# First blocks of a sliding-window attention and MLP kernel: q and k loaded and turned by batch, g applied at the copy of xT, w1 loaded ahead of two v blocks

## The chip, the cores and the metric

The kernel runs on one core of a Trainium2 chip. The metric is the device time of one execution in microseconds; the time of a kernel is the median of several runs. All times in the text are microseconds unless marked otherwise, and times of events are counted from the start of the profiled span.

## The reference

Inputs are q, k and v of shape (8, 8, 576, 64) (batch, heads, positions, head size), a gain g of 512 numbers, and two weights, w1 (512 x 2048) and w2 (2048 x 512), all f32.

```python
scores = scale * np.matmul(q, k.transpose(0, 1, 3, 2))
rel = pos[:, None] - pos[None, :]
slopes = 2.0 ** (-8.0 * (np.arange(H) + 1) / H)
bias = slopes[:, None, None] * (-np.abs(rel))[None]
mask = (rel >= 0) & (rel < 128)
scores = np.where(mask, scores + bias[None], -1e9)
attn = softmax(scores)                      # over the keys
x = (attn @ v).transpose(0, 2, 1, 3).reshape(B, S, 512)
mu, var = mean(x), variance(x)              # over the 512 columns
xn = (x - mu) / np.sqrt(var + 1e-6) * g_ln
out = x + np.maximum(xn @ w_ch1, 0.0) @ w_ch2
```

## The kernel before

The batches are taken in four pairs. A pair has nine blocks of 128 rows: blocks 0 to 7 alternate between the two batches of the pair (block 2i + b holds positions 128i to 128i + 127 of batch b), and block 8 holds the last 64 positions of both. The 36 blocks form twelve groups for the MLP, six of two blocks and six of four (`GROUPS`). A block passes through these stages:

- *Load.* `load_qk` and `load_v` issue DMAs from GpSimd's queue that also convert f32 to f16. For the first pair the q and k of blocks 2i and 2i + 1 come as one tile `raw`, batch 0 in the lower 64 partitions and batch 1 in the upper 64, by one DMA each of 128 KB. The list `loads` fixes their order; `load_until` issues them as far as a step asks for. w1 comes in eight chunks of 256 columns (`load_w1`), w2 in four.
- *Turn.* q and k are transposed on TensorE in 64x64 pieces (`transposed`, line L297), and copied from PSUM to the tiles `q` and `k`. Later pairs are turned by DMA instead.
- *Scores.* `attend` (L425) multiplies q by the keys of the own and the preceding block of the same batch into one of two score banks (`ps_sc`); ScalarE takes the exponential (L434), VectorE multiplies by a mask with the decay (L445).
- *Values.* `values` (L479) multiplies by v with a column of ones, in two halves of four heads; VectorE takes the reciprocal of the sums and scales (L487, L488), which gives x, and the sum of each row.
- *Centre and turn x.* `centre` subtracts the mean. For blocks 0 to 3 it also multiplies by g, with g spread over all partitions in `g_row` (L554); for later blocks it only subtracts (L563). `turn_x` transposes the result on TensorE (L575) and copies it into the group's `xT` (L576), by ScalarE or VectorE as the step says.
- *MLP.* `mlp1` runs 16 units, each four matmuls with a 128-column slice of w1 (L737) and an eviction with relu by ScalarE (L753) or, for the units listed, by VectorE (L745). Unit u of the first groups takes columns 128u to 128u + 127, so chunk c of w1 serves units 2c and 2c + 1. Groups 0 and 1 (blocks 0 to 3) use plain `w1`, since g is already in x; later groups use `w1g`, made by VectorE from w1 and g (`gain_w1`, L163). `mlp2` multiplies by w2 (L770), and `finish` scales by the inverse standard deviation and adds x.

`g_row` comes from `turn_first`: g is loaded as one line of 512, spread over 128 partitions by a matmul of a line of ones (`spread_g`, L284, tile `ps_g`), and copied out of PSUM by VectorE (L364).

The order is written out by hand: the engines run in the program's order. `steps` is a list of small steps; the steps before `first` run ahead of the MLP, and `weave_at` puts later ones between the units of `mlp1` and `mlp2`: a place u means that one step is taken after unit u. `warm(n)` puts n matmuls of ones (L279) into TensorE's queue; their result is not used.

```python
steps = warm_step(11) + [[(turn_first,)]] + warm_step(3)
steps += [scores_step(0), scores_step(1) + masks_of(0) + masks_of(1)] + warm_step(6)
...
weave_at(mlp1(0, (0, 1)), 0, 1, 2, 3, 6, 7, 8, 12)
weave_at(mlp1(1), 2, 8, 12)
weave_at(mlp2(0, ((0, 8), (8, 12), (12, NFB))), 0, 1, 3, 4, 4, 5)
```

During `mlp1(1)` the steps are the statistics of blocks 0 to 3 (`variance_of`, with `inv_std` at the end) and 13 of the 16 instructions of `gain_w1`; the first step in `mlp2(0)` is the turn of blocks 4 and 5 ("turn(4)"), whose two copies on VectorE stand behind them.

Of the kernel before, what the change touches and what calls it, by code (L numbers as in the profile page):

```python
# [10 lines left out]
FP16 = mybir.dt.float16  # L11
# [6 lines left out]
P = 128  # L18
# [41 lines left out]
def kernel(  # L60
# [154 lines left out]
    def load_qk(src, tag, p, i):  # L215

        n = min(P, S - i * P)
        t = raw_pool.tile([P, H, 2, D], FP16, tag=tag, name=tag)
        raw[tag, p, i] = t
# [28 lines left out]
    weights = {3: w1s + w2s[:2], 5: w2s[2:] + [(load_distances,)]}  # L248
    loads, place = [], []
    for n, (p, blk) in enumerate(order):  # L250
        for src, tag in ((q, "q"), (k, "k")):
            sooner = tag == "q" and 0 < blk < T and by_dma(p, blk // 2)
            if blk % 2 == 0 and not sooner:
# [27 lines left out]
    def spread_g():  # L281

        ps = ps_mm.tile([P, DM], FP32, tag="mm", name="ps_g")
        nc.tensor.matmul(ps, one_line, g_line, start=True, stop=True)  # L284
        return ps

    def transposed(tag, p, i, ps):


        st = raw.pop((tag, p, i))  # L290
        for hp in range(HP):
            for r in range(2):
                for b, dst in enumerate(ps):
# [9 lines left out]
    def turn(p, i, in_sc=False, copies=(nc.vector.tensor_copy, nc.scalar.copy)):  # L303
# [16 lines left out]
        if i < 4:  # L320
            transposed("q", p, i, [t[:, 0] for t in ps])
            if p == 0 and i == 1:
                warm(3)
# [216 lines left out]
    def centre(p, blk):  # L540
# [28 lines left out]
    def turn_x(g, at, p, blk, copy):  # L569
# [6 lines left out]
        copy(out=xT[:, :, at * P : (at + 1) * P], in_=ps)  # L576
# [371 lines left out]
    nc.vector.memset(one_line, 1.0)  # L948
# [59 lines left out]
```

## Time and profile before

| | us |
|---|---|
| median of three runs | 307.76 (307.71 to 307.97) |
| the profiled execution | 306.61 |
| its span | 304.8 |
| TensorE busy | 296.6 |
| VectorE busy | 218.7 |
| ScalarE busy | 171.8 |
| GpSimd busy | 145.7 |
| first matmul of `mlp1(0)` | 17.84 |

PE is TensorE's matmuls and PEld its loads of weights, DVE is VectorE, ACT ScalarE, POOL GpSimd and SP the queue of the sync engine. In the timeline a row gives the start, the time taken, the engine, the line, the operation, output and inputs by their names, shapes, and the number of instructions merged; in brackets stands the idle time before it and what ended it. In the chain in order of time a row is a piece of the one chain of work that ended last. A row of the DMA view gives what is loaded, the queue, the number, the size and the time from issue to landing. GpSimd's DMA rows show the writing of descriptors, not the transfer.

### The profile page before, as it was taken

To read this page: it belongs to the slowest core of one execution; us is meant where nothing else is said; L and a number is where in the kernel's file an instruction comes from. 1 tells how busy PE (TensorE), PEld (TensorE's weight loads), DVE (VectorE), ACT (ScalarE), POOL (GpSimd) and SP (SyncE) were. 2 spreads that over 40 slices of the span, in tenths; PEclk is the share of its full clock that TensorE was granted. 3 is DMA by queue.
4 is the path that set the end of the run, shared out by engine and by line. 5 is a ranking of instruction groups with operands and counts; after the bars stand their busy time and mean duration, and the time that the engine had idled before them with its cause. 6 is when DMAs were issued, how large, how long until landed. Compare 5 with 4: busy or idle time off the path is not lost.

```text
span 304.8 us, 8795 instructions
## 1 busy us (share of the span) xinstructions
PE 296.6 (97%) x3625; PEld 199.2 (65%) x3625; DVE 218.7 (72%) x529; ACT 171.8 (56%) x302; POOL 145.7 (48%) x195
## 2 busy tenths in 40 slices
PE   8999999999999999999999999999999999999994
PEld 2468755856758576546865686568657864784583
DVE  2689778867688778757994899489858985760463
ACT  5598776768758476387248624762586257305600
POOL 8964658936399757535875357508210321000001
PEclk9999999999999999999999999999999999999998
DMA  9999999999999999999999999998752050021004
GB/s 96 163 196 202 189 184 158 192 129 139 177 162 134 152 147 139 154 183 146 119 162 215 134 118 152 141 178 68 148 109 54 19 156 19 18 88 69 2 0 138
DMA packets 160186, 39.25 MB, mean 129 GB/s; under 512 B 149073, under 2 KB 155729, under 8 KB 160146
## 3 DMA queue, kind: packets, MB, share of 16 engines
q0 software_dynamic: 109744, 18.65, 86.8%
q1 hardware_dynamic: 50178, 19.71, 41.4%
q8 instruction: 28, 0.46, 0.7%
q10 hardware_dynamic: 224, 0.33, 0.3%
q14 instruction: 12, 0.10, 0.2%
HBM read 36.97 MB, written 9.44 MB: 152 GB/s over the span
## 4 chain that ended last, share of the span: by engine, by line
PE 86%; DVE 5%; DMA 5%; ACT 1%; issue 1%; POOL 1%; DVEq 0%; POOLq 0%
PE ps_r L737 28%; PE ps_r L836 24%; PE ps_m L737 10%; PE ps_m L770 10%; PE ps_sc L425 5%; DMA xT<-xc 3%; PE ps_r L479 3%; PE ps_warm L279 2%; DMA out_dram<-o 2%; PE ps_pv L479 2%; PE ps_sc L297 1%; DVE x L488 1%; PE ps_tx L575 1%; DVE o L854 1%; POOL rstd L538 0%
## 5 line engine op out<-in xcount | busy, mean ns | idle before, releaser
L737 PEld LDWEIGHTS <-w1g 128*128 128x128 f16 x640 | 61.0, 98 | 48.5 <-issue 0.9
L737 PE MATMUL ps_r<-xT,w1g 128*128 128x512 f16 x384 | 84.8, 379 | 0.0
L434 ACT ACTIVATE probs<-ps_sc 128x1024 f16<-128x1024 f32 x56 | 54.3, 1023 | 51.0 <-PE ps_sc L425 51.0
L753 ACT ACTIVATE ht<-ps_r 128x512 f16<-128x512 f32 x96 | 56.1, 600 | 32.0 <-PE ps_r L737 31.8
L535 POOL TENSOR_TENSOR rstd<-moments,powers 128x1 f32<-128x1 f32 x28 | 13.8, 492 | 84.3 <-DVE moments L581 84.2
L770 PE MATMUL ps_m<-w,ht 128*128 128x512 f16 x192 | 45.3, 380 | 0.0
L836 PE MATMUL ps_r<-w,ht 128*128 128x256 f16 x384 | 43.9, 273 | 0.0
L836 PEld LDWEIGHTS <-ht 128*128 128x128 f16 x384 | 37.2, 98 | 4.7
L240 POOL DMA_DIRECT2D vx<-in_v_dram x40 | 34.9, 883 | 10.3 <-DMA k<-in_k_dram 3.5
L753 ACT ACTIVATE ht<-ps_m 128x256 f16<-128x256 f32 x91 | 33.1, 389 | 7.8 <-PE ps_m L737 4.9
L737 PE MATMUL ps_m<-xT,w1g 128*128 128x256 f16 x256 | 30.4, 273 | 0.8 <-ACT ht L753 0.6
L227 POOL DMA_DIRECT2D q<-in_q_dram x30 | 25.6, 859 | 9.5 <-DMA vx<-in_v_dram 5.8
L770 PEld LDWEIGHTS <-ht 128*128 128x128 f16 x192 | 17.3, 98 | 18.2
L227 POOL DMA_DIRECT2D k<-in_k_dram x30 | 25.8, 870 | 5.8 <-DMA q<-in_q_dram 3.9
L445 DVE TENSOR_TENSOR probs<-probs,m 128x1024 f16<-128x1024 f16 x44 | 27.8, 672 | 0.0
L580 DVE BATCH_NORM_STATS2 st<-x 128x6 f32<-128x512 f16 x36 | 24.8, 689 | 0.7
L538 POOL TENSOR_TENSOR rstd<-rstd,powers 128x1 f32<-128x1 f32 x28 | 22.7, 811 | 2.2
L487 DVE RECIPROCAL rec<-ps_r 128x4 f32<-128x4 f32 x36 | 6.3, 176 | 22.4 <-PE ps_r L479 22.3
L836 PE MATMUL ps_r<-w,hs 128*128 128x256 f16 x192 | 21.9, 273 | 0.0
L479 PEld LDWEIGHTS <-probs 128*128 128x128 f16 x448 | 18.7, 97 | 4.8 <-DVE probs L445 0.5
L854 DVE TENSOR_TENSOR o<-ps_r,o 128x512 f32<-128x512 f32 (+1 forms) x25 | 16.6, 666 | 5.5 <-PE ps_r L836 5.1
L836 PEld LDWEIGHTS <-hs 128*128 128x128 f16 x192 | 18.8, 98 | 2.2
(86 smaller groups left out, 361.9 us busy)
## 6 DMA issues: line engine op xcount, KB each, us to landing
out_dram<-o SPq DMA_DIRECT2D x22, 256.0 KB, 5.0
q<-in_q_dram POOLq DMA_DIRECT2D x32, 128.0 KB, 9.5
k<-in_k_dram POOLq DMA_DIRECT2D x32, 128.0 KB, 9.5
vx<-in_v_dram POOLq DMA_DIRECT2D x32, 128.0 KB, 9.3
out_dram<-o SPq DMA_DIRECT2D x24, 128.0 KB, 4.7
w<-in_moe_w_ch_dram POOLq DMA_DIRECT2D x8, 256.0 KB, 8.4
w<-in_moe_w_ch_dram POOLq DMA_DIRECT2D x4, 512.0 KB, 10.7
q<-in_q_dram POOLq DMA_DIRECT2D x8, 64.0 KB, 5.9
```

The lines of the kernel that those rows point to most:

```text
L227: nc.gpsimd.dma_start(out=dst, in_=rows.rearrange("h p d -> p h d"))
L240: nc.gpsimd.dma_start(out=vx[p0 : p0 + n, :, 0:D], in_=v[b, :, t0 : t0 + n, :].rearrange("h p d -> p h d"),)
L434: nc.scalar.activation(out=dst.rearrange("p (n j) q -> p j n q", j=2), in_=ps.rearrange("p j n t q -> p j n (t q)"), func=AF.Exp, scale=in ...
L445: nc.vector.tensor_tensor(out=dst, in0=dst, in1=mask, op=ALU.mult)
L479: nc.tensor.matmul(ps[:, i, :], pr[:, h, t, :], vext[(p * NSLOT + o) % NV][:, h, :], start=(n == 0), stop=(n == len(terms) - 1),)
L538: nc.gpsimd.tensor_tensor(out=here, in0=here, in1=powers[:, 1:2], op=ALU.pow)
L580: nc.vector.bn_stats(out=st, in_=xs[order[n]])
L737: nc.tensor.matmul(ps[:, 0:cols], w[:, kb, fb * P : (fb + 1) * P], xT[:, kb, 0:cols], start=(kb == 0), stop=(kb == NKB - 1),)
L753: nc.scalar.activation(out=ht[:, fb, 0:cols], in_=ps[:, 0:cols], func=AF.Relu)
L770: nc.tensor.matmul(sums[at], ht[:, fb, at * P : (at + 1) * P], w2[:, fb, :], start=(fb == 0), stop=(fb == NFB - 1),)
L836: nc.tensor.matmul(banks[name][pair][:, pair, :], lhs[:, fb, pair * P : (pair + 1) * P], rhs[:, fb, :], start=(first and fb == 0 and (pair ...
L854: nc.vector.tensor_tensor(out=o[:, at, cols], in0=banks[name][at.start][:, at, :], in1=(x if to_x else o)[:, at, cols], op=ALU.add,)
```

## The change

Four things change, all in the work on blocks 0 to 3.

1. `load_qk` can load one batch of a tile. The q and k of blocks 0 and 1 are loaded in the order q of batch 0, k of batch 0, q of batch 1, k of batch 1, and turned in that order by `turn_part` and `copy_part`, each batch in its own score bank. Blocks 2 and 3 are turned in two parts, q and then k. The steps of the head are written anew, with 29 warm-ups in place of 35.
2. `spread_g`, the line of ones and the load of g as a line are gone. `centre` only subtracts the mean; `turn_x` multiplies by g while it copies: on VectorE with one `tensor_tensor`, on ScalarE with four activations with a scale by partition. Block 0 is copied by ScalarE, blocks 1, 2 and 3 by VectorE (before: block 1 by VectorE, the others by ScalarE).
3. The first three chunks of w1 are loaded ahead of v of block 2, the fourth ahead of v of block 3, the other four behind it as before.
4. `mlp1(0)` has units 0 to 3 evicted by VectorE (before: 0 and 1), and nine steps woven in at other units (one half of the scores of block 2 moves behind `first`).

```diff
-    spread = hsum[1].rearrange("p f d -> p (f d)").bitcast(FP32)
-    g_line, g_row = spread[:, 0:DM], spread[:, DM : 2 * DM]
-    g_line = g_line[0:1]
-    nc.sync.dma_start(out=g_line, in_=moe_g_ln.rearrange("(o d) -> o d", o=1))
-    one_line = consts.tile([1, P], FP32)
...
-    def load_qk(src, tag, p, i):
+    def load_qk(src, tag, p, i, bs=range(2)):
...
-        for b in range(2):
+        for b in bs:
             nc.gpsimd.dma_start(
                 out=t[b * n // 2 : (b + 1) * n // 2],
...
-    weights = {3: w1s + w2s[:2], 5: w2s[2:] + [(load_distances,)]}
-    loads, place = [], []
+    weights = {3: w1s[4:] + w2s[:2], 5: w2s[2:] + [(load_distances,)]}
+    loads, place = [(load_qk, src, tag, 0, 0, (b,)) for b in range(2) for src, tag in ((q, "q"), (k, "k"))], []
...
+        loads += {2: w1s[:3], 3: w1s[3:4]}.get(n, [])
         loads.append((load_v, p, blk))
...
-    def turn_first():
-
-        q, k = queries(0, 0), keys_tile("k", 0, 0)
-        ps = [bank(b)[:, 0] for b in range(2)]
-        transposed("q", 0, 0, ps)
-        for b in range(2):
-            nc.vector.tensor_copy(out=q[:, b], in_=ps[b])
-        ps_row = spread_g()
-        warm(2)
-        ps = [bank(b)[:, 0] for b in (0, None)]
-        transposed("k", 0, 0, ps)
-        for b, copy in enumerate((nc.scalar.copy, nc.vector.tensor_copy)):
-            copy(out=k[:, b].rearrange("p h (c r) -> p r h c", r=2), in_=ps[b])
-        nc.vector.tensor_copy(out=g_row, in_=ps_row)
+    def in_score_bank(tag, b):
+
+        junk[b] = True
+        return ps_sc[b][:, "qk".index(tag)].bitcast(FP16).rearrange(
+            "p (t r h c) -> p t r h c", t=2, r=2, h=HP
+        )[:, 0]
+
+    def turn_part(tag, i, bs):
+
+        if (tag, 0, i) not in turned:
+            queries(0, i) if tag == "q" else keys_tile(tag, 0, i)
+        transposed(tag, 0, i, [in_score_bank(tag, b) for b in bs], bs[0])
+
+    def copy_part(tag, i, b, copy):
+        t, ps = turned[tag, 0, i][:, b], in_score_bank(tag, b)
...
+        copy(out=t, in_=ps)
...
-        if p == 0 and blk < FIRST:
-            nc.vector.scalar_tensor_tensor(
-                out=xc,
-                in0=xs[p, blk],
-                scalar=mean,
-                in1=g_row,
-                op0=ALU.subtract,
-                op1=ALU.mult,
-            )
-        else:
-            nc.vector.tensor_scalar(
-                out=xc, in0=xs[p, blk], scalar1=mean, scalar2=None, op0=ALU.subtract
-            )
+        nc.vector.tensor_scalar(
+            out=xc, in0=xs[p, blk], scalar1=mean, scalar2=None, op0=ALU.subtract
+        )
...
-        copy(out=xT[:, :, at * P : (at + 1) * P], in_=ps)
+        dst = xT[:, :, at * P : (at + 1) * P]
+        if g >= FIRST_GROUPS:
+            copy(out=dst, in_=ps)
+        elif copy == nc.vector.tensor_copy:
+            nc.vector.tensor_tensor(
+                out=dst,
+                in0=ps,
+                in1=g_sb.unsqueeze(2).broadcast_to([P, NKB, P]),
+                op=ALU.mult,
+            )
+        else:
+            for kb in range(NKB):
+                nc.scalar.activation(
+                    out=dst[:, kb], in_=ps[:, kb], func=AF.Copy, scale=g_sb[:, kb : kb + 1]
+                )
...
-    steps = warm_step(11) + [[(turn_first,)]] + warm_step(3)
-    steps += [scores_step(0), scores_step(1) + masks_of(0) + masks_of(1)] + warm_step(6)
-    steps += values_steps(0)
-    steps += warm_step(2) + [turn_step(2, True, (nc.scalar.copy, nc.scalar.copy))]
-    steps += values_steps(1) + warm_step(4)
-    steps += [x_step(0, nc.scalar.copy)] + warm_step(2) + [scores_step(2)]
-    steps += [x_step(1) + [(warm, 2)] + masks_of(2, 1)]
+    steps = warm_step(8) + part_step("q", 0, 0, on_dve) + warm_step(1)
+    steps += part_step("k", 0, 0, on_dve) + warm_step(3) + [scores_step(0)]
+    steps += part_step("q", 0, 1, on_dve) + warm_step(1) + part_step("k", 0, 1, on_act)
+    steps += warm_step(4) + [masks_of(0) + scores_step(1)]
+    (rows0, rows0b), (rows1, rows1b) = values_steps(0), values_steps(1)
+    steps += [rows0, rows0b[:1] + masks_of(1)] + warm_step(5) + [rows0b[1:]]
+    steps += [rows1, rows1b[:1], [(turn_part, "q", 1, (0, 1))]]
+    steps += [[(copy_part, "q", 1, b, on_act) for b in range(2)], x_step(0, on_act)]
+    steps += [rows1b[1:]] + warm_step(2) + [[(turn_part, "k", 1, (0, 1))]]
+    steps += [[(copy_part, "k", 1, b, on_act) for b in range(2)]] + warm_step(2)
+    steps += [x_step(1)] + warm_step(3) + [[(scores, 0, 2, (0,))]]
...
-    steps += [[(scores, 0, 3, (0,))] + masks_of(2), [(scores, 0, 3, (1,))], products[0]]
+    steps += [[(scores, 0, 2, (1,))] + masks_of(2, 1), [(scores, 0, 3, (0,))] + masks_of(2)]
+    steps += [[(scores, 0, 3, (1,))], products[0]]
     steps += [centring[0][:1] + masks_of(3) + centring[0][1:], products[1]]
-    steps += [centring[1], x_step(2, nc.scalar.copy), x_step(3, nc.scalar.copy)]
+    steps += [centring[1], x_step(2), x_step(3)]
...
-            weave_at(mlp1(0, (0, 1)), 0, 1, 2, 3, 6, 7, 8, 12)
+            weave_at(mlp1(0, (0, 1, 2, 3)), 2, 3, 4, 5, 5, 8, 9, 11, 14)
```

`part_step(tag, i, b, copy)` is a step that calls `turn_part` and `copy_part` for one batch.

More of the change, by code (lines that the diff above doesn't have):

```diff
@@ L213, in by_dma @@
         return (p, i) >= BY_DMA_TURN
-    def load_qk(src, tag, p, i):
+    def load_qk(src, tag, p, i, bs=range(2)):
         n = min(P, S - i * P)
-        t = raw_pool.tile([P, H, 2, D], FP16, tag=tag, name=tag)
-        raw[tag, p, i] = t
+        if 0 in bs:
+            raw[tag, p, i] = raw_pool.tile([P, H, 2, D], FP16, tag=tag, name=tag)
+        t = raw[tag, p, i]
         if by_dma(p, i):
@@ L252 @@
             sooner = tag == "q" and 0 < blk < T and by_dma(p, blk // 2)
-            if blk % 2 == 0 and not sooner:
+            if blk % 2 == 0 and not sooner and n > 0:
                 loads.append((load_qk, src, tag, p, blk // 2))
+        loads += {2: w1s[:3], 3: w1s[3:4]}.get(n, [])
         loads.append((load_v, p, blk))
@@ L279, in warm, with transposed @@
             nc.tensor.matmul(ps, ones[:, 0:P], ones, start=True, stop=True)
[L281 to L290, printed above, removed]
+    def transposed(tag, p, i, ps, first=0):
+        st = raw[tag, p, i]
         for hp in range(HP):
             for r in range(2):
-                for b, dst in enumerate(ps):
+                for b, dst in enumerate(ps, first):
                     rows = slice(b * HALF, (b + 1) * HALF)
@@ L321, in turn @@
             transposed("q", p, i, [t[:, 0] for t in ps])
-            if p == 0 and i == 1:
-                warm(3)
             transposed("k", p, i, [t[:, 1] for t in ps])
@@ L349, in keys_tile @@
         return t
[L351 to L364 removed]
+    def in_score_bank(tag, b):
[9 more added lines that the diff above has]
+        t, ps = turned[tag, 0, i][:, b], in_score_bank(tag, b)
+        t = t.rearrange("p h r c -> p r h c" if tag == "q" else "p h (c r) -> p r h c", **({} if tag == "q" else dict(r=2)))
+        copy(out=t, in_=ps)
     ring = []
@@ L649, in warm_step, with part_step @@
         return [[(warm, n)]]
-    steps = warm_step(11) + [[(turn_first,)]] + warm_step(3)
-    steps += [scores_step(0), scores_step(1) + masks_of(0) + masks_of(1)] + warm_step(6)
-    steps += values_steps(0)
-    steps += warm_step(2) + [turn_step(2, True, (nc.scalar.copy, nc.scalar.copy))]
-    steps += values_steps(1) + warm_step(4)
-    steps += [x_step(0, nc.scalar.copy)] + warm_step(2) + [scores_step(2)]
-    steps += [x_step(1) + [(warm, 2)] + masks_of(2, 1)]
+    on_dve, on_act = nc.vector.tensor_copy, nc.scalar.copy
+    def part_step(tag, i, b, copy):
+        return [[(turn_part, tag, i, (b,)), (copy_part, tag, i, b, copy)]]
+    steps = warm_step(8) + part_step("q", 0, 0, on_dve) + warm_step(1)
[9 more added lines that the diff above has]
+    steps += [x_step(1)] + warm_step(3) + [[(scores, 0, 2, (0,))]]
     first = len(steps)
     products, centring = zip(*((h[0], h[1]) for h in map(values_steps, (2, 3))))
-    steps += [[(scores, 0, 3, (0,))] + masks_of(2), [(scores, 0, 3, (1,))], products[0]]
+    steps += [[(scores, 0, 2, (1,))] + masks_of(2, 1), [(scores, 0, 3, (0,))] + masks_of(2)]
+    steps += [[(scores, 0, 3, (1,))], products[0]]
     steps += [centring[0][:1] + masks_of(3) + centring[0][1:], products[1]]
-    steps += [centring[1], x_step(2, nc.scalar.copy), x_step(3, nc.scalar.copy)]
+    steps += [centring[1], x_step(2), x_step(3)]
     steps += [variance_of(0) + variance_of(1), variance_of(2) + variance_of(3)]
@@ L947 @@
     nc.vector.memset(magic, 0x5F3759DF)
-    nc.vector.memset(one_line, 1.0)
     nc.vector.memset(powers[:, 0:1], EPS)
```

## Prediction

> **What bounds the kernel now.** I read the page first: the busy shares and the chain.
>
> ```profile
> PE 296.6 (97%) x3625; PEld 199.2 (65%) x3625; DVE 218.7 (72%) x529; ACT 171.8 (56%) x302; POOL 145.7 (48%) x195
> ...
> PE 86%; DVE 5%; DMA 5%; ACT 1%; issue 1%; POOL 1%; DVEq 0%; POOLq 0%
> ```
>
> TensorE is the bound. The change touches only the 27.8 us before the second group's first product (`mlp1(1)`); from there on the built order of every engine is the same. So the question is how much earlier TensorE starts `mlp1(1)`, and whether VectorE and the loads follow. Second, the chain in order of time, at the start:
>
> ```profile
> 1.46 4.69 PE ps_warm L279 x11
> ...
> 6.53 1.05 PE ps_g L284 x2
> ...
> 9.32 0.45 PE ps_sc L425 x16
> ...
> 17.27 0.44 DVE xT L576
> ...
> 17.84 0.60 PE ps_m L737 x4
> ```
>
> No DMA stands in it: the head runs warm-ups, `ps_g`, turns, scores and values until `mlp1(0)` starts at 17.84. Third, the timeline and the time to landing of single loads of w1 (the first chunk, issued at 10.31, and the last, at 16.18):
>
> ```profile
> 10.31 4.58 POOL L156 DMA_DIRECT2D w<-in_moe_w_ch_dram  x6
> ```
> ```profile
> w<-in_moe_w_ch_dram POOLq DMA_DIRECT2D x1, 256.0 KB, 6.3
> ```
> ```profile
> 16.18 0.74 POOL L156 DMA_DIRECT2D w<-in_moe_w_ch_dram  x1 [0.17 <-issue]
> ```
> ```profile
> w<-in_moe_w_ch_dram POOLq DMA_DIRECT2D x1, 256.0 KB, 9.8
> ```
>
> The first chunk lands at 16.6, the last (columns of units 14 and 15) at 16.18 + 9.8 = 25.95 or so. Fourth, the timeline at the end of the stage:
>
> ```profile
> 26.24 0.39 PE L575 MATMUL ps_tx<-iden,xc 128*128 128x128 f16 x4
> 26.46 8.46 PE L737 MATMUL ps_m<-xT,w 128*128 128x256 f16 x76
> ```
> ```profile
> 26.02 0.69 DVE L580 BATCH_NORM_STATS2 st<-x 128x6 f32<-128x512 f16 x1
> ...
> 31.06 3.88 DVE L163 TENSOR_SCALAR w1g<-w,g_sb 128x512 f16<-128x512 f16 x13
> 36.50 0.43 DVE L326 COPY q<-ps_sc 128x512 f16<-128x512 f16 x1 [1.57 <-PE ps_sc L297]
> ```
>
> The 76 matmuls are unit 13 onward, 8.46/76 = 0.11 us each, 0.436 a unit. So unit 14 starts at 26.46 + 0.436 = 26.90, only 0.95 after its weights landed, and `mlp1(1)` at 26.46 + 3 x 0.436 = 27.77. VectorE works without a break from 26.02 to 34.93 and then idles 1.57 before the copies of turn(4).
>
> **The change part by part.**
>
> *Loads.* q and k of pair 0 go by batch (q0 k0 q1 k1), three w1 chunks go ahead of v of block 2, one ahead of v of block 3. GpSimd issues the same 24 loads up to the last w1 chunk, in about 0.7 to 0.9 us each as now; only their order differs. In the windows the queue moves 60 GB/s to 4.5 us (filling), then 148, 176 and 200: from 4.5 us it always has loads in hand, so the 24th load, the last w1 chunk, should land where it lands now. Chunks land 1.0 to 1.7 apart around a mean of 1.34, so I allow 0.35 either way. Chunk 0 no longer stands behind two v loads (issued at 8.57 and 9.44, landed at 15.0 and 15.9): it lands near 14.7, but chunk 4 stays at 21.9. Eight loads are in flight at most; the order of the waits on older loads changes, but each load is issued 8 to 10 us before it lands, as now, so nothing starves. The g line's 2 KB load on SP goes; nothing queues behind it there until the first store.
>
> *Head.* Batch 0's k is now the second load: issued near 2.05, landing between the first load (4.84) and the third (6.99), about 5.9. Then 16 transposes (0.3), the strided copy (0.72, row k L363) and hops bring scores(0) to 7.1 in place of 9.32. From there to `mlp1(0)` the present order takes 17.84 - 9.32 = 8.5; laying out the new one with the rows' durations (exp 1.02, masks 0.69, copies 0.58 and 0.73, the second batch's turn after its k lands at 8.0) I get 8.7, so `mlp1(0)` starts near 15.8, two us earlier. `ps_g` (1.05 on the chain), its 0.68 VectorE copy and six of 35 warm-ups go; they are part of those two us, not added to them.
>
> *g at the copy of xT.* Blocks 0 to 3 lose the product with the g row: 0.75 (L554) becomes a subtraction, 0.35 to 0.77 with a mean of 0.54 (L563): -0.2 on VectorE each. Block 0's copy on ScalarE becomes four instructions of 128x128; nearest rows are m_tail (0.20 from start to start) and the 128x256 relu (0.39): 0.8 to 1.6 against 0.59; I take 0.9, and it lies in the head. Blocks 1, 2, 3 become a VectorE product from PSUM. The trace has no such form with f16 in and a broadcast f32; the nearest are the plain copy, 0.42, and the 128x512 sum from PSUM with an f32 operand, 0.68 (L854); `scalar_tensor_tensor`, 0.75. I take 0.68, since that row too reads two operands, one from PSUM. For blocks 2 and 3 the copy moves from ScalarE to VectorE.
>
> *Where the head's two us go.* Units 0 to 7 run earlier, but unit 8 needs chunk 4 (21.9) and unit 14 the last chunk. TensorE waits there. Unit 14 then starts at 25.95 + 0.05 (as k at 8.00 to the transposes at 8.05) = 26.00. Block 3's transposes now follow unit 14, not unit 12: 26.00 + 0.44 = 26.44, ended at 26.83 (0.39), VectorE from 26.87 to 27.55 (0.68), and `mlp1(1)`, which needs block 3's columns, starts at 27.60. Unit 15 is over at 27.09, so TensorE idles 0.5. **Gain: 27.77 - 27.60 = 0.17.** By a copy of 0.42 it would be 0.43; by 0.75, 0.10. With 0.35 on the landing either way: +0.25 (slower) to -0.78.
>
> *What is late next.* VectorE's unbroken run now starts after block 3's product, at 27.46 in place of 26.02. It has the same 8.9 us of statistics and gains, so it is free at 36.37. The copies of turn(4) were awaited by scores(4) and started at 36.50; with TensorE 0.17 earlier they are wanted at 36.33. The idle 1.57 just covers the 1.44, short by 0.04. Two more evictions on VectorE (0.42 each) lie in units 2 and 3, ahead of the w1 wait. Beyond, w2's third part lands at 38.2 and is used at 40.2, so a shift of 0.2 meets no load.
>
> Sum against the profiled execution: 306.61 (span 304.8 and 1.81 around it) - 0.17 + 0.04 = 306.5. The median of the runs, 307.76, is 1.15 above that execution; the same sum there gives **307.6**, with 307.0 to 308.0 for this case. About 0.2%, 0.62 us, is what a measurement of this kernel can tell from no change, so this case is "the same".
>
> **The rivals.**
>
> *The runs have a longer head than the profile (faster).* In the profile warm-ups start every 0.43 us up to 5.70 and every 0.22 from 7.5: TensorE's clock doubled near 5.8, just ahead of `ps_g`. If the doubling comes later in the timed runs, `ps_g` and the warm-ups behind it cost up to 1.1 more, on the chain. That would be the 1.15 between median and profile. The new head has no `ps_g`, and a head up to 1 us later still meets the wait on w1. Gain 1.15 + 0.17: 306.4. For it: the size of the difference; against: nothing shows where it lies, and three runs agree within 0.26. The Trainium skill ("TensorE: Matmul & The Clock Gate", Part 1: The HAM clock gate) states that the clock is released after a busy window of about 3.4 us that runs freely, so that the moment varies from run to run; this trace's 4.4 us from first matmul to release fits that, and its one execution can't show the variation.
>
> *The last w1 chunk lands earlier (faster).* If the early queue had room and w1's larger rows fill it, every 0.1 is worth 0.1; at half a us the sum is 307.76 - 0.17 - 0.5 = 307.1, and beyond 0.95 nothing more comes of it. For: 60 GB/s in the first 4.5 us; against: those first six loads are of the same sizes and issue times as now.
>
> *The clock stays at half (slower).* The head has 8 warm-ups before the first turn, 3.4 us, not 11, and waits of 0.2 to 0.9 between them. If the clock doubles only at 12 us, 14 further warm-ups cost 0.43 and not 0.22, 2.9 in all, of which 0.75 falls into waits: `mlp1(0)` at 18.0. Then w1 no longer sets it: 18.0 + 9.93 (the present length of the stage) + 0.35 (one more half of scores in it) + 0.25 (block 3's copy) = 28.5, +0.75: 308.5. It decides from about 10 us on. Against: gaps of 0.4 in the present head cost no clock. By that same section, which asks for one wholly busy window, the shorter run of warm-ups could miss it; the trace neither shows nor excludes that.
>
> *VectorE late at turn(4) (slower).* The cover is 0.04 short; if the 13 gains ran at their slowest row (0.48, not 0.30) VectorE would be 2.3 late, 309.9; at half of that, 308.7. It must be 0.8 late to be seen.
>
> **How the numbers follow.** w1 gate as summed 0.40; longer head in the runs 0.25; earlier landing 0.15; clock 0.10; VectorE 0.10. Faster 0.40, same 0.40, slower 0.20. The range runs from 306.4, the first rival, to 308.5, the clock; what it leaves out is most of VectorE's case and the far ends of the others.
>
> **What would show it.** Right: TensorE waits for DMA of w before units 8 and 14, `mlp1(0)` starts near 15.8, `mlp1(1)` near 27.6 behind the xT of VectorE, VectorE's idle before turn(4) has shrunk from 1.57 to nothing. Wrong: the last w1 chunk lands away from 25.95; the product from PSUM is not 0.68; warm-ups at 0.43 after 7 us; or `mlp1(1)` moves by 0.2 and the end by more.

## The result, and the profile after

The changed kernel is slower by 0.35%, little but clear of the noise: 308.78 (median of 22 runs, 307.22 to 310.24) beside 307.60 for the kernel before (22 runs, 306.98 to 308.27); the ratio is 1.0035, with a 95% interval of 1.0020 to 1.0049. The forecast was 307.6, with a range of 306.4 to 308.5.

The median hides how the runs lie. Seven of the 22 stand at 307.22 to 307.75 (mean 307.52), none between 307.75 and 308.50, and fifteen at 308.50 to 310.24 (mean 309.19). All count as undisturbed, and the granted clock of the two groups is the same, 0.997 to 1.0. So a third of the runs took the time of the forecast and two thirds took 1.7 more; 307.52 + 15/22 x 1.67 = 308.66 is the mean that the ratio sees, beside 307.58 before. The profiled execution, 307.75 with a span of 306.0, is one of the lower group. It has to be read together with one of the other group, which was profiled later (`look_3`, below).

First the profile of the lower group. The chain of work that ended last, in order of time (start, duration, what):

```profile
5.02 0.46 PE ps_sc L288 x16
...
7.24 0.42 PE ps_sc L417 x16
...
14.93 9.22 DMA w<-in_moe_w_ch_dram
24.15 0.28 issue
24.44 9.49 DMA k<-in_k_dram
...
34.20 3.30 DVE w1g L158 x10
37.50 0.33 DVE q L315
37.83 0.65 DVE k L316
38.52 0.64 PE ps_sc L417 x32
```

Before, no DMA stood in this part. Now the chain runs over a load of w1, and VectorE's gains lead without a break into the copies of turn(4). TensorE's timeline in the stage:

```profile
22.89 0.61 PE L743 MATMUL ps_m<-xT,w 128*128 128x256 f16 x4 [0.52 <-DMA w<-in_moe_w_ch_dram]
...
26.94 0.61 PE L743 MATMUL ps_m<-xT,w 128*128 128x256 f16 x4 [0.36 <-DMA w<-in_moe_w_ch_dram]
27.39 0.39 PE L557 MATMUL ps_tx<-iden,xc 128*128 128x128 f16 x4
27.61 0.60 PE L743 MATMUL ps_m<-xT,w 128*128 128x256 f16 x4
28.56 2.68 PE L743 MATMUL ps_m<-xT,w 128*128 128x256 f16 x23 [0.35 <-DVE xT L562]
```

These are the waits that were forecast: for chunk 4 ahead of unit 8 (22.89), for the last chunk ahead of unit 14 (26.94), for the product with g ahead of `mlp1(1)` (28.56). Only the hour is other: the last chunk landed at 26.89, not at 25.95, from the row of its issue at 16.81 and its time to landing:

```profile
w<-in_moe_w_ch_dram POOLq DMA_DIRECT2D x1, 256.0 KB, 10.1
```

So `mlp1(1)` starts 0.79 later than before (28.56, 27.77), and VectorE with it:

```profile
27.81 0.69 DVE L562 TENSOR_TENSOR xT<-ps_tx,g_sb 128x512 f16<-128x512 f16 x1 [1.46 <-PE ps_tx L557]
28.42 0.68 DVE L576 BATCH_NORM_STATS2 st<-x 128x6 f32<-128x512 f16 x1
...
33.41 4.09 DVE L158 TENSOR_SCALAR w1g<-w,g_sb 128x512 f16<-128x512 f16 x13
37.42 0.41 DVE L315 COPY q<-ps_sc 128x512 f16<-128x512 f16 x1
```

The idle 1.57 ahead of the copies of turn(4) is gone: the copy starts as the last gain ends.

Second, the upper group. `look_3` is the same kernel, profiled later at 309.69 (span 307.9). TensorE's timeline, first the profile above and then `look_3`:

```profile
1.46 3.33 PE L276 MATMUL ps_warm<-ones 128*128 128x512 f16 x8 [1.46 <-DVE vx L952]
...
6.35 0.82 PE L276 MATMUL ps_warm<-ones 128*128 128x512 f16 x3
...
8.80 1.04 PE L276 MATMUL ps_warm<-ones 128*128 128x512 f16 x4
...
10.39 1.24 PE L276 MATMUL ps_warm<-ones 128*128 128x512 f16 x5
```
```profile
1.46 3.59 PE L276 MATMUL ps_warm<-ones 128*128 128x512 f16 x8 [1.46 <-DVE vx L952]
...
6.83 1.46 PE L276 MATMUL ps_warm<-ones 128*128 128x512 f16 x3
...
10.37 1.89 PE L276 MATMUL ps_warm<-ones 128*128 128x512 f16 x4
...
13.20 1.61 PE L276 MATMUL ps_warm<-ones 128*128 128x512 f16 x5
```

The same four warm-ups take 1.04 in the one and 1.89 in the other. From start to start a warm-up takes 0.40 to 0.43 until 4.0 and 0.21 to 0.23 from 6.4 on in the first; in `look_3` it takes 0.38 to 0.43 until 13.6 and 0.21 to 0.23 from 14.0 on. The 16 transposes behind the opening run tell the same: 0.44 at 5.02 in the first, 0.63 at 5.10 in `look_3`. So TensorE's clock, read from these lengths, doubled some nine us later. `mlp1(0)` starts at 19.18 in place of 16.44. No chunk of w1 is waited for then, and `mlp1(1)` starts at 30.00, 2.2 later than in the kernel before. The starts of `mlp1(0)` in the first profile and in `look_3`, and of `mlp1(1)` in `look_3`:

```profile
16.44 1.48 PE L743 MATMUL ps_m<-xT,w 128*128 128x256 f16 x12
```
```profile
19.18 1.05 PE L743 MATMUL ps_m<-xT,w 128*128 128x256 f16 x8
...
30.00 1.27 PE L743 MATMUL ps_m<-xT,w 128*128 128x256 f16 x10 [0.35 <-DVE xT L562]
```

The page's row of the granted clock does not tell the two apart; it stands at 9 from the first slice in both:

```profile
PEclk9999999999999999999999999999999999999999
```

### The profile page after: what moved, and what is told of

Its sections match the earlier page's. It is cut to its first block, busy times and chain, and to the rows that moved or that the text cites. A ratio compares the mean times of both kernels' runs of the same rounds, so it can differ in the third digit from the quotient of the medians.

```text
span 306.0 us, 8778 instructions
## 1 busy us (share of the span) xinstructions
PE 295.1 (96%) x3617; PEld 199.4 (65%) x3617; DVE 218.9 (72%) x531; ACT 170.9 (56%) x301; POOL 147.0 (48%) x195
## 4 chain that ended last, share of the span: by engine, by line
PE 79%; DMA 10%; DVE 6%; ACT 1%; POOL 1%; issue 1%; DVEq 0%; POOLq 0%
PE ps_r L743 27%; PE ps_r L842 24%; PE ps_m L776 12%; PE ps_sc L417 5%; PE ps_m L743 5%; DMA k<-in_k_dram 3%; DMA w<-in_moe_w_ch_dram 3%; DMA k<-k 3%; PE ps_r L471 3%; PE ps_pv L471 2%; ACT probs L426 1%; DMA q<-in_q_dram 1%; DVE w1g L158 1%; DVE x L480 1%; PE ps_sc L288 1%
## 5 line engine op out<-in xcount | busy, mean ns | idle before, releaser
L759 ACT ACTIVATE ht<-ps_m 128x256 f16<-128x256 f32 x89 | 32.4, 390 | 9.9 <-PE ps_m L743 7.4
L576 DVE BATCH_NORM_STATS2 st<-x 128x6 f32<-128x512 f16 x36 | 24.8, 689 | 0.7
L530 POOL TENSOR_TENSOR rstd<-rstd,powers 128x1 f32<-128x1 f32 x28 | 23.4, 835 | 2.2
L426 ACT ACTIVATE own<-ps_sc 128x1024 f16<-128x1024 f32 x12 | 12.0, 1022 | 16.2 <-PE ps_sc L417 15.7
L417 PE MATMUL ps_sc<-q,k 64*64 64x128 f16 (+1 forms) x1088 | 20.1, 208 | 0.5 <-DVE k L316 0.3
```

The costliest lines, as they stand in the source:

```text
L417: nc.tensor.matmul(at_q, kt[rows, hp, cols], of_q, start=True, stop=True,)
L426: nc.scalar.activation(out=dst.rearrange("p (n j) q -> p j n q", j=2), in_=ps.rearrange("p j n t q -> p j n (t q)"), func=AF.Exp, scale=in ...
L530: nc.gpsimd.tensor_tensor(out=here, in0=here, in1=powers[:, 1:2], op=ALU.pow)
L576: nc.vector.bn_stats(out=st, in_=xs[order[n]])
L759: nc.scalar.activation(out=ht[:, fb, 0:cols], in_=ps[:, 0:cols], func=AF.Relu)
```

## The experiments

Three theories were to be told apart. **Clock:** eight opening warm-ups are too short a run of TensorE to double the clock early in every execution, and an execution in which it doubles late is some two us longer. **Landing** (theory 1 in the expectations): the head's gain is lost because TensorE now waits for w1, whose last chunk lands later, by the order of the loads (theory A) or by chance (theory B). **Product** (theory 2): the product with g on VectorE and VectorE's later run cost the time. The clock theory was formed after the first eight kernels of this section; for those, landing and product were the two. The same kernel again stands first, though its last profile came last.

**The same kernel again** (`again`, `look_1`, `look_2`, `look_3`), with no edit.

> The changed kernel itself, once more, for a second landing of each chunk of w1. Theory A (the load order makes the last chunk late): the last chunk lands at 26.9 +- 0.2 again, `mlp1(1)` starts at 28.5, ratio to the kernel before 1.003 to 1.005. Theory B (the 0.95 is chance of one execution, the slowest of the 16 DMA engines): the landing moves by half a us or more, towards 25.95, `mlp1(1)` moves with it, and the profiled time with both.

Measured: the last chunk landed at 26.34 and `mlp1(1)` started at 28.01, half a us earlier than in the first profile, yet the span is 305.9, beside 306.0 there. Ratio 1.0011 (0.9988 to 1.0034), nine runs of twelve below 308.5, three at 309.06 to 310.13. So the landing moves from execution to execution (B), the end does not follow it one for one, and the ratio depends on how many runs fall in the upper group.

> The changed kernel again, one profile. Clock theory: either the warm-ups take 0.22 from 7 us at the latest, `mlp1(0)` at 16.3 to 16.8 and a time of 307.0 to 308.0, or they take 0.43 until about 13.5, `mlp1(0)` at 19.0 to 19.5, `mlp1(1)` at 29.9 to 30.3 and a time of 308.8 to 310.2; no profile with an early clock and a time above 308.5. Landing theory: the time follows the last chunk's landing, not the clock.

> The changed kernel once more, one profile, with the same two outcomes: clock released by 7 us and 307.0 to 308.0, or near 13.5 and 308.8 to 310.2.

> The changed kernel once more, with timed runs. Clock theory: the profile shows either a release by 7 us and 307.0 to 308.0, or near 13.5 and 308.8 to 310.2; of the timed runs a quarter to two thirds lie above 308.5, the rest at 306.9 to 308.3; ratio 1.001 to 1.005. Landing theory: one broad group around the landing of the last chunk.

`look_1` and `look_2` had the early clock: 307.57 and 307.97, `mlp1(0)` at 16.82 and 16.39, `mlp1(1)` at 27.74 and 28.26. In all four early profiles of this kernel the clock doubled between 4.0 and 5.8: the single warm-up that starts at 5.3 to 5.8 takes 0.39, in `look_3` 0.61. `look_3` is the late one shown above; its last chunk landed at 26.53, earlier than in the first profile, and the execution is 1.94 longer. Of its twelve timed runs four lie above 308.5 and eight at 306.91 to 308.44; ratio 1.0009 (0.9987 to 1.0032). Of all 48 runs of the changed kernel 22 lie from 308.5 up, and the two repeats with timed runs, 1.0011 and 1.0009, are not told from the kernel before.

**The kernel before again** (`again_before`).

> The kernel before itself, for a second profile. So far the mean over the 16 DMA engines of the last w1 chunk's end lies between 24.92 and 25.34 in every profile, whatever the order of the loads, while its slowest engine ended at 25.94 in the kernel before and at 26.03 to 26.89 in the others. If the slowest engine is chance (theory B): 26.0 to 26.9 here too, `mlp1(1)` still at 27.8 to 28.0, as unit 14 reaches the chunk only at 26.90. If the order of the changed kernel makes it late (theory A): 25.9 to 26.0 again. The span: 305.0 to 306.5, where its timed runs lie, as that first profile (304.8) was among the fastest of them; a ratio of 1.

Measured: the last chunk landed at 26.60, not 25.94; the mean end over the sixteen DMA engines is 24.94, as it was 24.92 in the first profile. `mlp1(1)` at 27.97, 306.80, ratio 0.9988 (0.9972 to 1.0004). The kernel before doesn't feel a late chunk, because its unit 14 comes only at 26.9. Theory A lost its main evidence here. What is left of it is small: over all 20 profiles of this section and the first two, the mean end is 24.89 in the old order of w1 and v (six profiles) and 25.10 in the new (fourteen). The slowest engine, which sets the landing, ends at 26.25 and 26.50 on average, a difference smaller than its changes within one order (25.82 to 27.02).

**No wait for the second half of w1** (`no_gate`).

```diff
-                    w[:, kb, fb * P : (fb + 1) * P],
+                    w[:, kb, (fb % 8 if g == 0 else fb) * P : (fb % 8 if g == 0 else fb) * P + P],
```

> Leaves out the second half of w1 in the first group's first product (units 8 to 15 read the columns of units 0 to 7), so that this group waits for no chunk after the fourth. Theory 1 (the gain of the head is lost in TensorE's waits for w1): the waits of 0.68, 0.17 and 0.53 before units 8, 12 and 14 go; block 3's product then waits for values(3) and the mask before it; `mlp1(1)` at 27.2 to 27.5 in place of 28.56 and 306.3 to 306.7 in a profile, 1.1 to 1.4 below the changed kernel. Theory 2 (the product with g on VectorE and VectorE's late run are what costs): less than 0.5 comes back, since the product stays where it is in the order.

Measured: this kernel leaves out half of w1 in the first group, so its time alone counts. The three waits are gone, `mlp1(1)` starts at 27.52, 1.04 earlier; block 3's product is still waited for, 0.51. But the profiled execution took 307.61, only 0.14 less, and four of ten runs lie above 308.5; ratio 1.0014 (0.9980 to 1.0049). The wait for w1 is real, but without it the end came only 0.14 earlier, and runs above 308.5 stay; it is not what puts them there.

**Block 3's turn two units earlier** (`x3_early`).

```diff
-            weave_at(mlp1(0, (0, 1, 2, 3)), 2, 3, 4, 5, 5, 8, 9, 11, 14)
+            weave_at(mlp1(0, (0, 1, 2, 3)), 2, 3, 4, 5, 5, 8, 9, 11, 12)
```

> Only the place of block 3's turn moves: behind unit 12, not 14, so it is off the path behind the last chunk. Theory 1: unit 14 still waits for its chunk (to 26.94 if that lands as before), then unit 15 and `mlp1(1)` follow without a gap at 27.8: 0.7 earlier than in the changed kernel, VectorE's statistics start near 27.1 in place of 28.42, scores(4) near 37.8; 307.0 to 307.2 in a profile. Theory 2: the same or more, up to 1.2, as the product on VectorE would be the whole of it. If neither: no change.

Measured, in TensorE's and VectorE's timeline:

```profile
25.47 0.40 PE L557 MATMUL ps_tx<-iden,xc 128*128 128x128 f16 x4
25.70 5.47 PE L743 MATMUL ps_m<-xT,w 128*128 128x256 f16 x46
```
```profile
25.33 1.28 DVE L562 TENSOR_TENSOR xT<-ps_tx,g_sb 128x512 f16<-128x512 f16 x2
26.52 0.68 DVE L576 BATCH_NORM_STATS2 st<-x 128x6 f32<-128x512 f16 x1
...
36.34 0.42 DVE L315 COPY q<-ps_sc 128x512 f16<-128x512 f16 x1 [1.04 <-PE ps_sc L288]
```

The wait for the product is gone, `mlp1(1)` starts at 27.30 and VectorE has 1.04 of idle time again ahead of turn(4). The profiled execution took 307.38, 0.4 less than the first of the changed kernel and 0.3 less than that of `again`; the ratio is 1.0012 (0.9994 to 1.0030), where `again` on the same chip has 1.0011. What the product theory blames is gone, and nothing that can be measured came back.

**The old order of q and k** (`qk_old`).

```diff
-    loads, place = [(load_qk, src, tag, 0, 0, (b,)) for b in range(2) for src, tag in ((q, "q"), (k, "k"))], []
+    loads, place = [(load_qk, src, tag, 0, 0, (b,)) for src, tag in ((q, "q"), (k, "k")) for b in range(2)], []
```

> The changed kernel with q and k of blocks 0 and 1 loaded in the old order (q0 q1 k0 k1). Theory 1: the head is 1.3 to 2 us longer (`mlp1(0)` at 17.8 to 18.5), but unit 14 still waits for the last chunk or misses it by at most half a us, so `mlp1(1)` stays at 28.5 to 29.0 and the time within 0.5 of the changed kernel: the two us of the head are worth nothing. Theory A for the order by batch: the last chunk lands at 25.95 again. A head that counts in full: 1.5 to 2 slower.

Measured: `mlp1(0)` at 19.46, no wait for w1 left, `mlp1(1)` at 30.28, 309.85; ratio 1.0042 (1.0012 to 1.0073), eight runs of twelve above 308.5. That is more than the order of two loads can do: scores(0) come 1.3 later than in the changed kernel, `mlp1(0)` 3.0 later. In its timeline the warm-ups take 0.43 until 13.5. This row began the clock theory, and it spoils the run as a test of the order.

**All of w1 behind v again** (`w1_behind_v`).

```diff
-    weights = {3: w1s[4:] + w2s[:2], 5: w2s[2:] + [(load_distances,)]}
+    weights = {3: w1s + w2s[:2], 5: w2s[2:] + [(load_distances,)]}
...
-        loads += {2: w1s[:3], 3: w1s[3:4]}.get(n, [])
```

> The changed kernel with all of w1 loaded behind v of blocks 2 and 3 again. Theory A: the last chunk lands at 25.95, `mlp1(1)` at 27.6, 0.6 to 0.9 below the changed kernel. Theory B: the last chunk lands at 26.0 to 26.9 as in any order, unit 0 waits for the first chunk (16.5 to 17.0, mlp1(0) 0.1 to 0.5 later) and the middle chunks as now; `mlp1(1)` at 27.6 to 28.6, 1.3 to 1.6 behind whatever the landing is; the time like that of the changed kernel within 0.3.

Measured: the last chunk landed at 25.82, the earliest of all, and still `mlp1(1)` starts at 30.00 and the execution takes 309.89; ratio 1.0028 (1.0006 to 1.0050). Its clock doubled at 13.5 to 13.9, too. Theory A had forecast 27.6.

**g at the copies alone, on the kernel before** (`g_copy`): `centre` and `turn_x` are those of the changed kernel, the line of g and its load are gone.

```diff
-        ps_row = spread_g()
...
-        nc.vector.tensor_copy(out=g_row, in_=ps_row)
...
-    steps += [centring[1], x_step(2, nc.scalar.copy), x_step(3, nc.scalar.copy)]
+    steps += [centring[1], x_step(2), x_step(3)]
```

> The second part of the change alone, on the kernel before: g at the copies of xT, no matrix product that spreads it, blocks 2 and 3 copied by VectorE; loads and order of steps of before. Theory 1 (the product costs only where it stands behind the last chunk): the head is up to 0.7 shorter, as k of batch 1 lands at 8.0 whatever stands ahead; block 3's product ends 0.25 later behind its transposes than the copy did, which the head's gain pays; `mlp1(1)` at 27.3 to 28.0; time within 0.3 of before. Theory 2 (the product on VectorE is what costs): `mlp1(1)` at 28.3 or later, scores(4) later by 0.7 or more, 1.002 to 1.004.

Measured: ratio 1.0006 (0.9993 to 1.0018), `mlp1(1)` at 28.14, inside the bound of theory 1 but for 0.14. scores(0) stay at 9.43 without `ps_g`: it had filled time in which batch 1's k was not there yet (TensorE now idles 0.61 for it). The head is not shorter, as was forecast, but longer: `mlp1(0)` starts at 18.47, 0.63 later than before, 0.44 of it idle time for the product of block 1. The product theory, which asked for 1.002 or more, falls.

**The interleaved kernel** (`interleaved`): half of mask(3) ahead of values(2), the turns of blocks 2 and 3 earlier, and two units of `mlp1(1)` ahead of units 14 and 15.

```diff
+    def both():
+        a, b = mlp1(0, (0, 1, 2, 3)), mlp1(1)
+        for it, n in ((a, 14), (b, 2), (a, 2), (b, 14)):
+            for _ in range(n):
+                yield next(it)
...
+            weave_at(both(), 2, 3, 4, 5, 5, 7, 8, 10, 11, 18, 24, 28)
```

> The changed kernel with other work put where TensorE waits: half of mask(3) ahead of values(2), values(3), the turns of blocks 2 and 3 one to three units earlier, and two units of the second group's first product ahead of units 14 and 15 of the first's. If theory 1 holds (1.4 us of waits for w1 and 0.5 for the product with g are what the head's gain turned into): the waits in this stage fall from 2.3 to 0.5-0.8, both first products end 1.4 to 1.8 earlier than in the changed kernel, VectorE starts its statistics at 26.5 to 27.0, and the time falls to 306.2-306.6, a ratio of 0.996 to 0.998. Theory 2: VectorE's product and its run behind it still set scores(4); at most 0.5 comes back. Where the end doesn't follow the stage at all (later waits take it up): no change.

Measured: ratio 1.0003 (0.9980 to 1.0025), and the profile again with the clock doubled only at 13.5 to 13.9, `mlp1(0)` at 19.07, 309.54. So three of the seven profiles with eight opening warm-ups had the late clock, and the next set asks why.

**Eleven opening warm-ups on the changed kernel** (`warm_11`), and **eight on the kernel before** (`before_8`): one number each.

```diff
-    steps = warm_step(8) + part_step("q", 0, 0, on_dve) + warm_step(1)
+    steps = warm_step(11) + part_step("q", 0, 0, on_dve) + warm_step(1)
```
```diff
-    steps = warm_step(11) + [[(turn_first,)]] + warm_step(3)
+    steps = warm_step(8) + [[(turn_first,)]] + warm_step(3)
```

> The changed kernel with 11 warm-ups ahead of the first turn, as the kernel before has, in place of 8: the one edit. Clock theory (the changed kernel's first unbroken run of TensorE, 1.46 to 4.43, is too short to release the clock in every execution: in three of seven profiles with that run the warm-ups still take 0.43 until 13.5, and these are 2.5 to 3 us late at `mlp1(0)`): the opening run ends at 6.1, scores(0) start at 8.0 to 8.3, `mlp1(0)` at 17.2 to 17.6, the last chunk is still the gate and `mlp1(1)` starts at 28.0 to 28.6; all warm-ups behind 6.1 take 0.22; the timed runs lie within 306.8 to 308.4, with no second group at 308.5 to 310.2; ratio 0.998 to 1.001. Landing theory (the lateness of w1 alone makes the changed kernel slower): the spread of the timed runs stays, 307.2 to 310.2, ratio 1.001 to 1.004 or higher, as the head is now longer.

> The kernel before with 8 opening warm-ups in place of 11: the one edit, nothing else of the change. Clock theory: in a part of the executions (a third to two thirds) the warm-ups still take 0.43 until 9 to 14; there `mlp1(0)` starts 1 to 2.7 later than 17.84 and `mlp1(1)` 1 to 2.7 later than 27.77; timed runs in two groups, near 307.5 and 308.5 to 310; ratio 1.000 to 1.006. Landing theory: three warm-ups less in the head change nothing or gain up to 0.5; one group of runs, ratio 0.998 to 1.000.

Measured: `warm_11` gives 1.0008 (0.9989 to 1.0027), early clock in its profile, `mlp1(0)` at 17.30, two runs of twelve above 308.5, where none was forecast. `before_8`, which has nothing of the change but three warm-ups less, gives 1.0050 (1.0019 to 1.0080): nine of its twelve runs lie at 309.55 to 311.01 and three at 306.89 to 308.38. Its timeline:

```profile
1.46 3.59 PE L279 MATMUL ps_warm<-ones 128*128 128x512 f16 x8 [1.46 <-DVE vx L946]
...
6.67 2.07 PE L284 MATMUL ps_g<-hs,one_line 1*128 1x512 f32 x2
...
10.21 1.46 PE L279 MATMUL ps_warm<-ones 128*128 128x512 f16 x3
11.60 1.07 PE L425 MATMUL ps_sc<-q,k 64*64 64x128 f16 x32
```

`ps_g` takes 2.07 (on the chain 2.00, where it took 1.05), scores(0) start at 11.60 in place of 9.32, `mlp1(0)` at 20.34 in place of 17.84. `before_8` decides: three warm-ups taken away, and nothing else, make the kernel before slower by as much as the whole change did in the first comparison, or more. `warm_11` alone is weak evidence, since the changed kernel itself came to 1.0011 and 1.0009 in its repeats. Taken together, the four kernels with the new head and ten or eleven opening warm-ups (`warm_11`, `inter_11`, `inter_11_v`, `inter_fill`) have 9 of 47 runs above 308.5, the kernel before beside them 11 of 64, and the changed kernel 22 of 48.

**Both cures together** (`inter_11`: `interleaved` with eleven opening warm-ups; `inter_11_v`: that with w1 behind v).

> The interleaved kernel with 11 opening warm-ups. Clock theory and theory 1 together: no execution keeps the slow clock, `mlp1(0)` starts at 17.2 to 17.6, TensorE's waits for w1 and for block 3's product are filled, both first products end 0.8 to 1.5 earlier than in the changed kernel's profile; 306.3 to 306.9, ratio 0.996 to 0.998. If only the clock counts and the stage doesn't: 307.3 to 307.6, ratio 0.999 to 1.0.

> As the last one, with all of w1 loaded behind v of blocks 2 and 3 again. In the four profiles with that order of the loads the mean end of the last w1 chunk over the 16 DMA engines was 24.77 to 24.97 and the slowest 25.82 to 26.60; in the six with w1 ahead of v 24.92 to 25.34 and 26.03 to 26.89. So it lands 0.3 to 0.4 earlier; `mlp1(0)` at 17.2 to 17.6 no longer needs the first chunk before 16.6. If the landing still counts in this order of steps: 0.1 to 0.4 below the last kernel. If the waits for w1 are filled there: the same within 0.15.

Measured: 1.0002 (0.9985 to 1.0020) and 1.0022 (1.0000 to 1.0044), `mlp1(0)` at 17.68 and 17.45, scores(4) at 38.19 and 37.96. No gain, where 0.996 to 0.998 was forecast for the first. With eleven warm-ups the new head brings `mlp1(0)` only 0.2 to 0.5 ahead of the old (17.84), and the stage behind it carries one more half of scores (0.35); that this is the reason was not tested. The last chunk of `inter_11_v` landed at 27.02, the latest of all, in the old order of the loads, where 0.3 to 0.4 earlier was forecast: chance again. Why four of eleven runs of `inter_11_v` lie above 308.5 is not settled; its profile has the early clock.

**What remained open** (`fill_8`: the changed kernel with one more warm-up in each of the three waits behind the opening run; `w1_first`: the kernel before with the new order of w1 and v alone; `inter_fill`: `interleaved` with ten opening warm-ups, filled waits and mask(1) earlier).

```diff
-    steps = warm_step(8) + part_step("q", 0, 0, on_dve) + warm_step(1)
-    steps += part_step("k", 0, 0, on_dve) + warm_step(3) + [scores_step(0)]
-    steps += part_step("q", 0, 1, on_dve) + warm_step(1) + part_step("k", 0, 1, on_act)
+    steps = warm_step(8) + part_step("q", 0, 0, on_dve) + warm_step(2)
+    steps += part_step("k", 0, 0, on_dve) + warm_step(4) + [scores_step(0)]
+    steps += part_step("q", 0, 1, on_dve) + warm_step(2) + part_step("k", 0, 1, on_act)
```

```diff
-    weights = {3: w1s + w2s[:2], 5: w2s[2:] + [(load_distances,)]}
+    weights = {3: w1s[4:] + w2s[:2], 5: w2s[2:] + [(load_distances,)]}
...
+        loads += {2: w1s[:3], 3: w1s[3:4]}.get(n, [])
         loads.append((load_v, p, blk))
```
```diff
...
-    steps += [rows0, rows0b[:1] + masks_of(1)] + warm_step(5) + [rows0b[1:]]
+    steps += [rows0 + masks_of(1), rows0b[:1]] + warm_step(3) + [rows0b[1:]]
...
```

> The changed kernel with its 8 opening warm-ups, and one more warm-up in each of the three waits of 0.35 to 0.41 that follow (ahead of k of batch 0, scores(0), k of batch 1). If those waits are what misses the release of the clock: warm-ups of 0.22 from 7 us at the latest, `mlp1(0)` at 16.4 to 16.8, timed runs in one group, 307.0 to 308.3, ratio 0.998 to 1.001. If it is the length of the first unbroken run: two groups as in the changed kernel, a third to two thirds of the runs above 308.5, ratio 1.001 to 1.005. Landing theory: as the changed kernel.

> The kernel before with the third part of the change alone: three chunks of w1 ahead of v of block 2, one ahead of v of block 3. Its opening run has 11 warm-ups. Clock theory: one group of runs, ratio 0.999 to 1.001. Landing: the last chunk lands at 26.0 to 26.9 in place of 25.9 to 26.6; unit 14 reaches it at 26.90 in this order of steps, so `mlp1(1)` stays at 27.8 to 28.0. If the order of the loads were what costs: `mlp1(1)` at 28.3 or later and 1.002 to 1.004.

> The interleaved kernel with 10 opening warm-ups, the three waits behind them filled with one warm-up each, and mask(1) put between the two halves of block 0's values, so that values(1) no longer wait 0.86 for it (two warm-ups less there). With a stable clock: scores(0) at 7.6 to 8.0, `mlp1(0)` at 16.2 to 16.8, the last chunk of w1 (26.0 to 26.9) still stands in front of units 14 and 15, and the second group's product has begun by then; scores(4) at 37.3 to 37.6 (37.61 in the kernel before): 307.0 to 307.5, ratio 0.997 to 0.9995. If the clock is missed all the same: a group of runs at 308.5 to 310.

Measured: `fill_8` 1.0014 (0.9991 to 1.0038), early clock in its profile, four runs of twelve above 308.5: fewer than in the first comparison, but no proof either way: whether the length of the opening run counts, or the waits behind it, stays open. `w1_first` 1.0003 (0.9977 to 1.0029), last chunk at 26.66, `mlp1(1)` at 27.59: the order of the loads alone costs nothing that can be measured in the time. `inter_fill` 1.0008 (0.9988 to 1.0028), `mlp1(0)` at 17.75. No version beats the kernel before.

All profiles together: of the twelve with eight opening warm-ups five doubled the clock late (between 11 and 14), and these took 309.54 to 309.89; of the eight with ten or eleven none did. Fourteen of the fifteen others took 306.61 to 308.77; `g_copy` took 308.88, with TensorE idle 1.59 ahead of 116.60 for VectorE. Of the timed runs of kernels with eight, 59 of 130 lie from 308.5 up; with ten or eleven 12 of 82; of the kernel before in all comparisons 18 of 171. A run above 308.5 is no proof of a late clock: `fill_8` (308.77) and `g_copy` had the early one. The timed runs leave no trace, so that the upper group of the first comparison is the late clock is inferred from the five profiles and from `before_8`, not seen run by run.

## Why the prediction was wrong, step by step

*The step that failed* is the head: it was laid out with durations from a trace whose clock had doubled near 5.8, and the case that it would not double was a rival with a chance of 0.10. The chance was mis-sized: five profiles of twelve had it, and by their times some two thirds of the runs of the first comparison. The argument against it, "gaps of 0.4 in the present head cost no clock", read the wrong thing: those gaps stand behind an unbroken run of 4.7 us (eleven warm-ups of 0.43), and the new head has them behind one of 3.4 (eight). The price was too small as well. It counted 14 slow warm-ups behind the opening run and had `mlp1(0)` at 18.0 and a time of 308.5; measured are eleven, 19.18 and a mean of 309.19 for the upper group. Of the 1.2 at `mlp1(0)`, 0.6 stands in the profile with the early clock, too (16.44, 15.8 forecast). The rest fits the other work of the head, which the sum left as it was and which slows down with the warm-ups: 16 transposes take 0.63 in place of 0.44. The Trainium skill, which the prediction named for this ("TensorE: Matmul & The Clock Gate", Part 1: The HAM clock gate), gives the window as 3.4 us that runs freely. The trace agrees that the moment varies: 4.0 to 5.8 in four executions of one kernel, 13.6 to 14.0 in a fifth. It does not agree that the window must be busy from end to end: in `again` and `x3_early` the warm-up that starts at 4.00 is followed by the next after 0.33 and 0.36, so the clock doubled at most 2.9 after the first matmul in the trace (1.46). How much idle time a window bears, and why a window was missed until 13.6, no run here shows.

*The first rival* looked for this variation in the kernel before, to explain why its median stood 1.15 above its profiled execution. It was the wrong kernel: all eight profiles with ten or eleven warm-ups have the early clock, in `w1_first` from 4.8 on. What that 1.15 consists of stays open.

*The loads.* "The last w1 chunk lands where it lands now, 25.95 ± 0.35" was a range around one sample. Over all 20 profiles the mean end of that transfer on the sixteen DMA engines lies at 24.8 to 25.4, and its slowest engine at 25.8 to 27.0. The first profile of the kernel before was among the lowest. The term was short by 0.5 on average. That the order of the loads does not matter was right for the time (`w1_first`); the mean end is 0.2 later in the new order. By the rows of its queue the last chunk is GpSimd's 20th load, not the 24th, which changes nothing in the sum.

*The mechanism of the forecast case* was right: waits ahead of units 8 and 14, the product at 0.69 (0.68 forecast), TensorE idle 0.51 for it (0.5), counted from the end of unit 15 at 0.436 a unit, `mlp1(1)` directly behind. In the four profiles of the changed kernel with the early clock `mlp1(1)` starts at 27.74 to 28.56, in place of 27.60; with a chunk at 26.5 in place of 25.95 it had come out at 28.15. The lower group of runs, 307.52, meets the forecast of 307.6, but this is partly luck: in the profile of that group `mlp1(1)` came 0.79 later than before and not 0.17 earlier, and that execution took 307.75 where the sum gave 306.5; the 1.15 that was added on top is what stays open above.

*The head otherwise.* scores(0) at 7.24 (7.1 forecast); `mlp1(0)` at 16.44 (15.8): values(1) wait 0.70 for their mask, which stands on VectorE behind the evictions of block 0's values, and ScalarE's four activations took 1.16 (0.9). With the early clock neither counts, as w1 is the gate.

*VectorE at turn(4).* The cover went as forecast; its price was 0.12 (TensorE idle 0.33 ahead of scores(4), before 0.21), 0.04 forecast.

## What to carry to other kernels

Warm-ups have a second task beside filling time. In these kernels ten or eleven at the start came with an early doubling of the clock in all eight profiles, and eight failed to in five profiles of twelve; one good profile shows nothing of that. Before an opening is shortened, take several profiles and read the spacing of equal matmuls, and look at how the timed runs lie before trusting their median or one trace. And before a long term is costed at "lands where it lands now", see how much that landing varies: slack that hid the variation before is spent as soon as the engine comes earlier.

## What was not expected of the hardware

The doubling of the clock moved between executions of the changed kernel from between 4.0 and 5.8 us to 13.6, with nothing between; four of the five late profiles have it at 13.5 to 14.0, `before_8` between 11.0 and 12.6. A transfer of 256 KB over sixteen DMA engines ended on the slowest engine 0.8 to 2.1 after the mean of all. And the end does not follow the stage: from `mlp1(1)` to the end the profiles of the changed kernel differ by 0.6, as single waits of TensorE come and go: 0.59 at 62.84 in the first, 0.87 at 62.71 in `look_1`, 0.64 at 115.05 in `again`. In `x3_early` this row on VectorE held TensorE for 0.88:

```profile
92.01 0.41 DVE L510 TENSOR_SCALAR xc<-x,moments,rstd 128x512 f16<-128x512 f16 x1 [1.53 <-POOL rstd L530]
```
